# Spectra kept by halves of the channels, products joined in pairs on VectorE, and other first loads, in a long convolution with a sparse feed-forward

## The chip, the cores and the metric

The kernel runs on one core of a Trainium2 chip. The metric is the device time of one execution in microseconds (us), smaller being better. The classes are "faster", "same" and "slower", with a border of 2%. All times below are medians of several executions; the profile is one execution, recorded by the hardware profiler, and its span is about 1.8 us shorter than the device time of that same execution (163.2 of 164.97 us).

## The reference

Two branches work on the same input of 2048 positions and 512 channels, and a gate mixes them. Branch A is a state-space convolution: a kernel of 2048 taps for each channel is built from 128 complex exponentials and applied through a Fourier transform. Branch B sends the two positions with the highest score through a small feed-forward.

```python
def _A_ref(u, A_re, A_im, B_re, B_im, C_re, C_im, log_dt, Dskip):
    dt = jnp.exp(log_dt)[:, None]
    A = A_re + 1j * A_im; Bc = B_re + 1j * B_im; Cc = C_re + 1j * C_im
    P = jnp.exp((dt * A)[:, :, None] * l[None, None, :])          # l = 0 .. 2047, in bfloat16
    K = jnp.einsum("dn,dnl,dn->dl", Cc, P, dt * Bc).real
    ...                                                            # pad to 4096, rfft of K and of u
    y = irfft(Uf * Kf)[..., :L]
    return y.transpose(0, 2, 1) + u * Dskip
def _B_ref(x, w_r, w_gate, w_up, w_down):
    idx = jnp.argsort(-(x @ w_r), axis=-1)[:, :2]
    ...                                                            # silu(xs @ w_gate) * (xs @ w_up) @ w_down, two rows
    return x + upd
x = A_u
g = _sigmoid((x * gate_w).sum(-1, keepdims=True))
return g * _A_ref(x, ...) + (1 - g) * _B_ref(x, ...)
```

## The kernel before

The kernel is written as a graph of named operations. A list scheduler in the program gives each operation an engine (`ENGINE` pins some of them) and a place in that engine's order, after the priorities in `ORDER`; the program is written out with each engine's list in that order. Both tables were searched for, not written by hand. The operations that the argument touches:

The first loads. The sync queue (SP) issues most of them, ScalarE (ACT) two small ones:

```python
g.dma("ld id", ..., writes=[bID], eng=ACT, first=0)      # identity
g.dma("ld ldt", ..., writes=[bLD], eng=ACT, first=1)     # log_dt
for i in range(3):
    for a in range(2):                                   # A_re A_im C_re C_im B_re B_im, all on SP
        g.dma("ld pn%d%s" % (a, "ACB"[i]), ..., 131e3, writes=[bPN[i][a]], first=2 + 2 * i + a)
...                                                      # then u, the transform matrices c_fwd
```

The spectrum X of the input: TensorE (PE) makes two rows at a time, ScalarE or VectorE (DVE) evicts them, VectorE spreads them to sums and differences. A row holds all 512 channels:

```python
def eov(b, ri, row, *dims):
    return tXE(BF, 0, 128, (4 * b + 2 * ri + 1) * 2048 + row * D, *dims)
...
g.op("ev X%d.%d.%d" % (b, ri, pr), {ACT: (... eov(b, ri, 2 * pr, (1, 1024)) ...), DVE: (...)}, bp, [bEO[b][ri][pr]], pref=ACT)
```

The taps of the convolution: decay tables (`t1_...`) are multiplied on VectorE, TensorE makes the taps from them ("tap", lines L898 and L899 of the profile), selections ("sel", L925) and the spectra of the kernel ("Kh", L958) follow, each evicted by ScalarE or VectorE. The products of the spectra come last. Each product of two real planes is one VectorE operation, and so is each sum of two terms; block 1 needs four products a part:

```python
def prod(nm, kb, kri, b, xri, ...):
    tt(nm, lambda: f4(t), lambda: k4(kb, kri), lambda: xw(b, xri), ALU.mult, bKH[...] + bX[b][xri], [bt], cd(NE), bias)
def comb(nm, a, b_, op, dst=None, NE=NE):
    tt(nm, ... a[0] ..., ... b_[0] ..., op, [a[1], b_[1]], [d[1]], cd(NE), bias)
...
ab.append((prod(nm + "a", 0, 0, blk, xs_[0]), prod(nm + "b", 0, 1, blk, xs_[1])))
...
comb(nm, ab[ri][0], ab[ri][1], ALU.subtract if ri == 0 else ALU.add, yds[ri] if blk == 0 else None)
if blk == 1:
    comb(nm + "cd", cd_[ri][0], cd_[ri][1], ALU.subtract if ri == 0 else ALU.add)
    comb(nm + "s", ab[ri][0], cd_[ri][0], ALU.add, yds[ri])
```

Behind them come the folds (VectorE), the inverse transform (TensorE, L1250 to L1254), and the outputs ("out", ScalarE or VectorE), which are stored.

## Time and profile before

| | kernel before |
|---|---|
| time, median of 3 executions | 163.63 us (163.33 to 163.76) |
| the profiled execution | 164.97 us, span 163.2 us |
| busy in it | TensorE and VectorE most: VectorE 149.9 us in 228 instructions |

The profiled execution took 1.2 us more than the longest timed one and 1.3 us more than their median. The lines on which the reading rests stand in the prediction. In a row of the stretches the columns are the bounds, the length, then busy time and number of instructions of PE, PEld (TensorE's weight loads), DVE, ACT and POOL, then the granted clock of TensorE as a share, the share of the DMA engines and GB/s.

### The profile page before, as it was taken

To read this page: it belongs to the slowest core of one execution; us is meant where nothing else is said; L and a number is where in the kernel's file an instruction comes from. 1 tells how busy PE (TensorE), PEld (TensorE's weight loads), DVE (VectorE), ACT (ScalarE), POOL (GpSimd) and SP (SyncE) were. 2 spreads that over 40 slices of the span, in tenths; PEclk is the share of its full clock that TensorE was granted. 3 is DMA by queue.
4 is the path that set the end of the run, shared out by engine and by line. 5 is a ranking of instruction groups with operands and counts; after the bars stand their busy time and mean duration, and the time that the engine had idled before them with its cause. 6 is when DMAs were issued, how large, how long until landed. Compare 5 with 4: busy or idle time off the path is not lost.

```text
span 163.2 us, 3756 instructions
## 1 busy us (share of the span) xinstructions
PE 146.2 (90%) x1574; PEld 102.4 (63%) x1574; DVE 149.9 (92%) x228; ACT 123.8 (76%) x242; POOL 4.2 (3%) x12
## 2 busy tenths in 40 slices
PE   0588899999799999849999999999999999999991
PEld 0443545464334457748555679998588888888880
DVE  0499999999999999999998999999999999999933
ACT  3698999999998998999998989974751602562352
POOL 5000000000000000000100000000000000000000
PEclk9999999999999999858999999999999999999999
DMA  4899600000000996596152504858000000044044
GB/s 148 257 378 416 209 7 0 4 4 0 0 0 3 324 352 227 187 349 242 39 222 38 221 4 159 359 181 335 2 0 6 0 0 4 0 129 133 0 129 129
DMA packets 13300, 21.19 MB, mean 130 GB/s; under 512 B 2018, under 2 KB 10980, under 8 KB 12516
## 3 DMA queue, kind: packets, MB, share of 16 engines
q1 hardware_dynamic: 12996, 20.93, 37.2%
q8 instruction: 12, 0.20, 0.5%
q10 hardware_dynamic: 288, 0.03, 0.1%
q14 instruction: 4, 0.03, 0.1%
HBM read 18.86 MB, written 2.10 MB: 128 GB/s over the span
## 4 chain that ended last, share of the span: by engine, by line
PE 57%; ACT 20%; DVE 16%; DMA 3%; SPq 1%; issue 1%; DVEq 0%
PE RP L1253 17%; PE RP L958 14%; DVE RB L664 10%; PE RP L788 6%; ACT RB L851 6%; ACT RB L768 5%; ACT RB L689 5%; PE RP L844 4%; PE RP L925 4%; DMA RB<-in_A_B_re_dram 3%; PE RP L1250 2%; ACT RB L990 2%; PE RP L1227 2%; PE RP L1147 2%; DVE RB L686 2%; PE RP L898 1%
## 5 line engine op out<-in xcount | busy, mean ns | idle before, releaser
L664 DVE TENSOR_TENSOR RB<-RB 128x2048 bf16<-128x2048 bf16 (+4 forms) x103 | 83.0, 870 | 1.3 <-ACT RB L792 0.8
L844 PE MATMUL RP<-RB 128*128 128x512 bf16 x128 | 31.3, 380 | 2.8 <-ACT RB L851 1.4
L1253 PE MATMUL RP<-RB 128*128 128x256 bf16 x256 | 32.0, 273 | 0.0
L1253 PEld LDWEIGHTS RP<-RB 128*128 128x128 bf16 x256 | 25.0, 98 | 3.0 <-issue 0.2
L958 PE MATMUL RP<-RB 128*128 128x256 bf16 x208 | 25.0, 273 | 0.0
L963 ACT ACTIVATE RB<-RP 128x1024 bf16<-128x1024 f32 x14 | 14.2, 1042 | 13.7 <-PE RP L958 13.7
L708 DVE TENSOR_TENSOR RB<-RB 128x2048 bf16<-128x2048 bf16 x20 | 23.8, 1218 | 0.1
L958 PEld LDWEIGHTS RP<-RB 128*128 128x128 bf16 x208 | 20.1, 98 | 4.5 <-issue 0.2
L844 PEld LDWEIGHTS RP<-RB 128*128 128x128 bf16 x128 | 11.7, 97 | 17.6 <-ACT RB L851 3.3
L1266 ACT ACTIVATE RB<-RP,RB 128x256 bf16<-128x256 f32 x28 | 10.8, 487 | 12.0 <-DVE RB L664 5.5
L792 ACT ACTIVATE RB<-RP 128x512 bf16<-128x512 int16 x32 | 18.4, 610 | 1.5 <-PE RP L788 1.3
L768 ACT ACTIVATE RB<-RP 128x256 bf16<-128x256 f32 x62 | 18.9, 507 | 0.0
L851 ACT ACTIVATE RB<-RP 128x1024 bf16<-128x1024 f32 x15 | 15.4, 1079 | 0.4 <-PE RP L847 0.3
L788 PE MATMUL RP<-RB 128*128 128x512 bf16 x56 | 15.5, 380 | 0.0
L898 PE MATMUL RP<-RB 128*128 128x84 bf16 x128 | 11.8, 213 | 3.5 <-DVE RB L664 3.1
L898 PEld LDWEIGHTS RP<-RB 128*128 128x128 bf16 x128 | 11.2, 105 | 4.0 <-DVE RB L664 3.2
L710 DVE TENSOR_TENSOR RB<-RB 128x1024 bf16<-128x1024 bf16 x20 | 13.4, 683 | 0.0
L899 PE MATMUL RP<-RB 128*128 128x84 bf16 x128 | 11.8, 212 | 0.0
L899 PEld LDWEIGHTS RP<-RB 128*128 128x128 bf16 x128 | 11.3, 105 | 0.0
L689 ACT ACTIVATE RB<-RB 128x512 bf16<-128x512 int16 x16 | 9.1, 626 | 0.5 <-DVE RB L686 0.5
L913 ACT ACTIVATE RB<-RP 128x1008 bf16<-128x1008 f32 x9 | 9.0, 1046 | 0.0
L1250 PE MATMUL RP<-RB 128*128 128x256 bf16 x32 | 8.8, 274 | 0.0
(106 smaller groups left out, 161.1 us busy)
## 6 DMA issues: line engine op xcount, KB each, us to landing
RB<-in_A_u_dram SPq DMA_DIRECT2D x4, 1024.0 KB, 6.0
RB<-c_kspec SPq DMA_DIRECT2D x6, 512.0 KB, 4.6
RB<-c_fwd SPq DMA_DIRECT2D x4, 512.0 KB, 9.1
RB<-c_inv SPq DMA_DIRECT2D x2, 1024.0 KB, 6.6
RB<-in_B_w_up_dram SPq DMA_DIRECT2D x2, 896.0 KB, 6.9
RB<-in_B_w_gate_dram SPq DMA_DIRECT2D x2, 896.0 KB, 6.0
RB<-in_B_w_down_dram SPq DMA_DIRECT2D x2, 896.0 KB, 6.1
out_dram<-RB SPq DMA_DIRECT2D x6, 256.0 KB, 2.4
```

The costliest lines, as they stand in the source:

```text
L664: return g.op(name, {DVE: (lambda h: h.tensor_tensor(out=o(), in0=a(), in1=b(), op=op), cost)}, rd, wr, bias=bias, **kw)
L689: s1.append(g.op("sin z%d.%d" % (t, hh_), {ACT: (lambda h, ta=ta, i=i, hh_=hh_: h.activation(out=tZ[hh_](BF, 0, 128, i * 512, (256, 2), (1 ...
L708: g.op("%s.m%d" % (name, i), {DVE: (lambda h, i=i: h.tensor_tensor(out=ts[i](BF, 0, 128, 0, (n, 2), *like), in0=a_(), in1=b_(i), op=ALU.mu ...
L768: e2.append(g.op("exp t1_%d %d" % (h, m), {ACT: (lambda hh, m=m, s=s, h=h: hh.activation(out=tT1[h](BF, 0, 128, s * 4, (128, NG), (1, 4)), ...
L788: r = hh.matmul(ps(F32, 0, 128, 0, (1, 512)), tAM(BF, 0, 128, 1 * 128, (1, 128)), tU8(BF, 0, 128, (x * 2 + h) * HC, (0, 2), (1, HC)), star ...
L792: sins.append(g.op("sin%d %d.%d" % (h, q, cs), {ACT: (lambda hh, ps=ps, cs=cs, tt_=tt_, q=q: hh.activation(out=tt_(BF, 0, 128, 8 * q, (4, ...
L844: r = h.matmul(o, tF(BF, 0, 128, (((eo * 2 + ri) * 4 + j // 2) * 4 + ft) * 128, (1, 128)), tU(BF, 0, 128, (b * 8 + j) * D, (1, D)), start= ...
L851: g.op("ev X%d.%d.%d" % (b, ri, pr), {ACT: (lambda h, ps=ps, b=b, pr=pr, ri=ri: h.activation(out=eov(b, ri, 2 * pr, (1, 1024)), in_=ps(F32 ...
L898: hh.matmul(o, tT1[h](BF, 0, 128, gr * 128, (1, 128)), t2v(h, 0, 0, (HC, NSL), (1, 4)) if gr == 0 else tT2[h](BF, 0, 128, 4 * gr, (HC, NSL ...
L899: r = hh.matmul(o, tTI[h](BF, 0, 128, gr * 128, (1, 128)), tT2[h](BF, 0, 128, NSL * HC + 4 * gr, (HC, NSL), (1, 4)), start=False, stop=True)
L958: r = hh.matmul(o, tKM[m](BF, 0, 128, c, (1, 128)), tKC[h](BF, 0, 128, u * 256, (1, 256)), start=(n == 0), stop=(n == len(steps) - 1))
L1253: r = hh.matmul(o, tG(BF, 0, 128, ((j * 2 + ri) * 4 + ft) * 128, (1, 128)), SD(hb, ri, ft), start=False, stop=(fin and k == 1 and ft == r0 ...
```

## The change

The intent is fewer VectorE instructions. The two products that a part needs from one kernel block become one operation of double length, and in block 1 the two first sums become one as well. For that the spectra X are kept by halves of 256 channels, so that real and imaginary planes lie at one step (positive for the real part of the product, negative for the imaginary). The first loads are reordered, and `ORDER`, `PLACE` and `ENGINE` are searched anew.

```diff
-        g.dma("ld id", ..., eng=ACT, first=0)
-        g.dma("ld ldt", ..., eng=ACT, first=1)
+        g.dma("ld id", ..., eng=ACT, first=1)
+        g.dma("ld ldt", ..., eng=ACT, first=0)
...
-                g.dma("ld pn%d%s" % (a, "ACB"[i]), ..., 131e3, writes=[bPN[i][a]], first=2 + 2 * i + a)
+                g.dma("ld pn%d%s" % (a, "ACB"[i]), ..., (131e3, 131e3, 200e3)[i], writes=[bPN[i][a]],
+                      eng=ACT if (i, a) == (2, 0) else SP, first=2 + 2 * i + a)
...
-            return tXE(BF, 0, 128, (4 * b + 2 * ri + 1) * 2048 + row * D, *dims)
+            return tXE(BF, 0, 128, (4 * b + 2 * ri + 1) * 2048 + row // 4 * 2048 + row % 4 * HC, *dims)
...
+                        tQ = T(nm, nt * NE * 4); bq = [Buf(tQ) for _ in range(nt)]
+                        for kb in range(nt):
+                            tt(nm + ("ab", "cp")[kb], lambda ...: tQ(BF, 0, 128, kb * 2 * NE, (NE, 2), (NE // 2, 2), (1, NE // 2)),
+                               lambda ...: tKH[h](..., (2048, 2), (4 * HC, 2), (1, NE // 2)),
+                               lambda ...: tXE(..., ((1 - 2 * ri) * 2048, 2), (4096, 2), (1, NE // 2)), ALU.mult,
+                               bKH[h][kb * 4:kb * 4 + 4] + bX[b][0] + bX[b][1], [bq[kb]], cd(2 * NE), bias)
...
+                                tt(nm, lambda qv=qv: qv(0), lambda qv=qv: qv(0), lambda qv=qv: qv(1), op, bq, bq, cd(2 * NE), bias)
+                                tt(nm + "s", yds[ri], ..., ALU.add, bq, [bY[ri]], cd(NE), bias)
...                                    # ORDER and PLACE: all new numbers
-    "ev Kh 0.0.2": DVE, "ev kc1": ACT, "ev X1.0.1": DVE, "ev tap 0.60": DVE, "ev tap 1.60": DVE, "x": DVE, ...
+    "ev Kh 0.1.3": DVE, "ev kc1": DVE, "ev kd0": DVE, "out 0.1.3": DVE, "ev X0.1.0": DVE, "ev X0.1.2": DVE, "x": ACT, ...
```

## The prediction

> **What bounds the kernel now.** I read the busy table by stretches first, then the chain that ended last, then the waits, then the groups by form and single rows of the timeline.
>
> The stretches (time, then busy time and instruction count of each engine, granted clock, DMA share, GB/s):
>
> ```profile
> 8.00:60.00 52.00, 48.26 (x332) 24.30 (x330) 51.64 (x93) 50.33 (x97) 0.31 (x1) 1.00 0.35 128
> 60.00:79.20 19.20, 15.56 (x340) 12.70 (x338) 19.06 (x30) 18.43 (x48) 0.73 (x3) 0.82 0.67 231
> 79.20:158.80 79.60, 79.58 (x884) 63.23 (x885) 75.78 (x102) 49.89 (x91) 0.83 (x3) 1.00 0.29 100
> 158.80:163.20 4.40, 0.83 (x8) 0.49 (x6) 1.75 (x4) 1.24 (x4) 0.00 (x0) 1.00 0.42 119
> ```
>
> The columns after the time are PE, PEld, DVE, ACT, POOL. VectorE works 51.64 of 52.00 us, then 19.06 of 19.20, then 75.78 of 79.60, and the missing 3.8 us of the last figure lie almost wholly behind its final fold at 156.24. ScalarE is as full up to 79 us and then has 30 us to spare. TensorE is not full before 79.2 us, and full after it: 79.58 of 79.60. So there are two bounds on top of each other: VectorE from 8 to 156 us, TensorE from 79.2 to 158.8 us. The chain says the same:
>
> ```profile
> 14.54 5.83 ACT RB L689 x11
> ...
> 63.17 4.41 DVE RB L664 x4
> ...
> 79.00 0.17 DVE RB L1142
> 79.22 3.19 PE RP L1147 x14
> ...
> 157.45 0.33 PE RP L1175 x8
> 157.78 0.99 PE RP L1253 x8
> 158.80 1.36 DVE RB L1271 x3
> 160.16 0.39 DVEq L533
> ```
>
> ScalarE carries it from 14.5 to 48 us, VectorE from 61 to 79, TensorE from 79.22 to 158.8 with no gap. Of the waits, three matter: TensorE for the decay tables that VectorE multiplies, before the first tap (L898); TensorE for a load at the start; VectorE for the first matmuls.
>
> ```profile
> PE RP L898 <- DVE RB L664: 3.1, 1, 3.1
> PE RP L621 <- DMA RB<-in_A_B_re_dram: 1.1, 1, 1.1
> DVE RB L644 <- PE RP L621: 1.1, 1, 1.1
> DVE RB L659 <- PE RP L621: 1.0, 1, 1.0
> ```
>
> What an instruction of VectorE costs, by form (busy us, mean ns) and in a row:
>
> ```profile
> L664 DVE TENSOR_TENSOR RB<-RB 128x2048 bf16<-128x2048 bf16 x49 | 58.0, 1218 | 1.1 <-ACT RB L792 0.6 <-ACT RB L963 0.3
> L708 DVE TENSOR_TENSOR RB<-RB 128x2048 bf16<-128x2048 bf16 x20 | 23.8, 1218 | 0.1
> L664 DVE TENSOR_TENSOR RB<-RB 128x512 bf16<-128x512 bf16 x32 | 12.0, 416 | 0.0
> L664 DVE TENSOR_TENSOR RB<-RB 128x1024 bf16<-128x1024 bf16 x16 | 10.4, 682 | 0.0
> ...
> 107.29 48.95 DVE L664 TENSOR_TENSOR RB<-RB 128x2048 bf16<-128x2048 bf16 x73
> ```
>
> From 682 to 1218 ns are 1024 elements more: 0.523 ns an element. The recorded fixed part, 682 - 1024 x 0.523 = 146 ns, overlaps the neighbour. What a row really pays is in the last line: 73 operations in 48.95 us (its shape is the first one's; it mixes 25 of 2048, 16 of 1024 and 32 of 512 elements, 83,968 together). At 0.521 ns that is 43.7 us of elements, so 5.2 us, or 70 ns an instruction, is the fixed price in a row. L708, whose operands already go in two planes with steps of both signs, has the same 1218 ns.
>
> [...] So joining instructions can save only the 70 ns; no element goes faster. [...] Here one issue on the sync queue takes 0.42 to 0.44 us, so a load moved away lets each later one start by about 0.45 us earlier. [...] a 3.1 us wait ahead of the taps, then 0.75 of the clock in 71 to 79 us.
>
> **The change part by part.**
>
> Products. Each real or imaginary part of a spectrum needs two products for a block, four for block 1. The new code makes the two in one operation of double length. Its first sums of block 1 are also one operation for both kernels' terms. Per pair of half and block:
> - half 0, block 0 and half 1, block 0: per part, two products and one sum become one product and one sum. 2 saved each, 4 together.
> - half 0, block 1: the imaginary part goes from 4 products and 3 sums to 2 and 2 (3 saved). The real part is summed in TensorE and goes from 4 products to 2 (2 saved). 5 together.
> - half 1, block 1: in three pieces, two parts each, 7 to 4 operations: 3 x 2 x 3 = 18 saved.
>
> Sum 27 instructions, so 27 x 0.070 = 1.9 us of VectorE; its elements stay. 1.3 us of it fall into the last block. In the last block VectorE's time (16 operations of 1024, 32 of 512) is 16 x 0.603 + 32 x 0.337 = 20.4 us before and about 19.1 after.
>
> All 27 lie behind about 91 us, where the Y products begin. There TensorE is full too. So by themselves they shorten nothing: TensorE's 79.6 us are the down projection, the remaining sine arguments, selections, kernel spectra, second taps, sums and inverses, and the diff takes no matmul away. The saving reaches the end only through the new order of operations, which is the largest part of the diff. VectorE's work ahead of the first taps includes things for later (the second half's tables, the spreads of X), and 1.9 us of it can be put off behind 79 us. Then the decay tables, and with them TensorE's full stretch, start earlier. ScalarE must keep pace, and it is full there. The assignment list relieves it by two early evictions of X that are now pinned to VectorE where there was one (1.08 us of ScalarE each, 1.21 of VectorE), but adds the copy "x" (0.6 us). So about half of the 1.9 us can be turned into an earlier 79.2: 0.9 to 1.0 us.
>
> Spectra by halves. The evictions of X write four runs of 256 instead of one of 1024, the TensorE add of the previous block reads two runs. Elements stay, I put this at 0. The spreads stay at 2048 contiguous elements.
>
> First loads. log_dt goes before the identity, so the exponential that VectorE and TensorE wait for (4.23 us, 4.97 us) can start up to 0.4 us earlier, but the identity, needed by the same product, comes 0.4 later. B_re goes from fifth on the sync queue (issue at 2.60, needed at 7.05) to third on ScalarE's, at about 1.6. B_im, U and the transform matrices each start some 0.45 us earlier. "x" on ScalarE gives VectorE 0.6 us in its idle start. The head is worth 0.4 to 0.6 us; I take 0.5.
>
> Sum: 163.6 - 1.0 - 0.5 = 162.1 us; I predict 162.1.
>
> **The rivals.**
> - TensorE as the only bound of the last half: VectorE's 1.9 us turn into idle time. For it: 79.58 of 79.60. Against: a wait of 3.1 us and the half clock sit just before that stretch, so its start can move. Then only the head counts: 163.1 us.
> - The whole saving lands: order and assignments were searched anew, VectorE gives 1.9 us, the head 0.5, and the taps meet a warm clock (up to 1.5 us more). For it: the two saturated engines have idle third partners (30 us of ScalarE behind 79). That makes 161.2, and with the clock 159.8.
> - Coarser operations start later: a joined product needs all four evictions of a kernel's spectrum and both parts of X, where one product needed two evictions and one part. The last eviction is about 1.1 us behind. For it: VectorE has waited for an eviction (L963, 0.3 us). Against: VectorE has other products to put in between nearly all the time. If it bites: +0.5 to 1 us, 163.5 to 164.
> - The negative step of the imaginary part's second operand costs the 2x rate. L708 speaks against it. If true, six to eight of the joined products double, over 10 us; I give it 1 in 100.
>
> **Range and chances.** The head is fairly sure, the rest depends on a search that I don't see. 8 in 10: 160.6 to 163.4. Two per cent is 160.4 us, which needs the full saving and the warm clock: 8 in 100. Slower by over 2% (166.9) needs a mistake in the rate: 2 in 100.
>
> **What would show it.** VectorE at about 199 instructions rather than 228, with tensor_tensor forms of 4096 elements at some 2.28 us; the same 0.52 ns an element; its total busy time down from 149.9 by 1 to 2 us. TensorE again without a gap from the down projection to the last inverse, with about 80 us, but starting near 78 rather than 79.2; B_re no longer on the chain. It is wrong if the last stretch of TensorE is itself shorter by a microsecond or more, if the 3.1 us wait before the taps is gone with the clock full, or if VectorE shows new waits for kernel-spectrum evictions.

Its sum: 163.6 - 1.0 - 0.5 = 162.1. Its 1.0 is the estimate of what half of 27 x 70 ns is worth, its 0.5 one from the times of the first loads; the 70 ns and the times are read from the trace. That joining leaves the time of an element as it is was the inference from rows of 512 to 2048 elements; the form of 4096 below has 0.521 ns. "The 2x rate" is the text's name for the 0.52 ns an element of the bf16 forms; with f32 operands the forms of 256 and 512 elements (L759 and L664, 417 and 678 ns) come to 1.02 ns, twice that. "The warm clock" is a granted clock of 1.00 in place of the 0.50 that its trace has from 68.1 to 74.9 us. The "up to 1.5 us" for it comes with no source there. The trace allows such an estimate: 48 taps start at that clock, one each 0.07 us, 3.3 us in all, and at the 0.039 us of the later taps they would take 1.9 us. That a shorter wait brings the full clock was an assumption, not shown.

## The result, and the profile after

| | median | runs | all runs |
|---|---|---|---|
| before | 163.63 us | 4 | 163.33 to 163.76 |
| after | 162.98 us | 4 | 162.91 to 163.25 |

The ratio is 0.9966, with a 95% interval of 0.9948 to 0.9983: "same". A ratio here is the mean time of one kernel's fast runs over that of the other's of the same rounds, so it is not quite the ratio of the medians. The gain is 0.65 us by these medians, and 0.46 us in a second measurement below, where 1.5 had been forecast. The time lies inside the range, but the gain was two to three times too large in the forecast.

The groups by form of the kernel after, VectorE's products and sums (count, busy us, mean ns, idle before):

```profile
L663 DVE TENSOR_TENSOR RB<-RB 128x2048 bf16<-128x2048 bf16 x37 | 44.2, 1219 | 1.0 <-ACT RB L791 0.9
...
L663 DVE TENSOR_TENSOR RB<-RB 128x4096 bf16<-128x4096 bf16 x9 | 20.2, 2287 | 0.0
...
L663 DVE TENSOR_TENSOR RB<-RB 128x1024 bf16<-128x1024 bf16 x16 | 10.3, 686 | 0.0
...
L663 DVE TENSOR_TENSOR RB<-RB 128x512 bf16<-128x512 bf16 x8 | 3.1, 420 | 0.1
```

The double-length form took 2287 ns. From 1219 to 2287 are 2048 elements more, 0.521 ns each, and the longest of the nine took 2290 ns: nothing was lost to the negative steps. VectorE has 201 instructions where it had 228, the 27 that the count gave. Its busy time fell only from 149.9 to 149.4 us, though: 27 instructions at 70 ns are 1.9 us, so some 1.4 us of other work has come to it over the whole kernel.

The same stretches as in the prediction, kernel after:

```profile
8.00:60.00 52.00, 47.42 (x337) 24.80 (x342) 51.42 (x93) 50.97 (x100) 0.59 (x2) 1.00 0.37 132
60.00:79.20 19.20, 15.52 (x327) 12.84 (x326) 19.13 (x27) 18.00 (x46) 0.60 (x3) 0.82 0.50 164
79.20:158.80 79.60, 78.20 (x881) 63.57 (x881) 76.12 (x79) 49.34 (x92) 0.62 (x2) 1.00 0.32 115
...
```

TensorE is done before the third stretch is over, and VectorE has more work in it than before (76.12 against 75.78 us) in 23 instructions fewer (79 against 102). The clock ahead of the taps is as low as it was (0.82). The chain that ended last, kernel after (start, length, what):

```profile
75.64 0.91 ACT RB L913
...
77.73 2.97 PE RP L1147 x13
...
155.66 1.87 PE RP L1236 x16
157.55 0.47 ACT RB L1249
...
```

The down projection (L1147) now follows an eviction of taps on ScalarE (L913), not VectorE. And its waits at the two places that the prediction named:

```profile
DVE RB L606 <- ACT RB L604: 3.8, 1, 3.8
...
PE RP L898 <- DVE RB L663: 2.6, 1, 2.6
```

The wait before the taps is 2.6 us where it was 3.1; no wait for B_re is left. VectorE's last operations, in the timeline of the kernel after (start, length, first of the group, idle before it and what ended it):

```profile
139.67 15.91 DVE L663 TENSOR_TENSOR RB<-RB 128x2048 bf16<-128x2048 bf16 x25
156.24 1.75 DVE L1254 TENSOR_SCALAR RB<-RP,RB 128x256 bf16<-128x256 f32 x4 [0.65 <-PE RP L1236]
```

Before its last outputs VectorE waits 0.65 us for TensorE; before the change that wait was 2.6 us (L1271 in the profile before, 156.24 to 158.80). The two engines end almost together now.

At face value the full stretch of TensorE starts 1.5 us earlier (77.73 against 79.22), more than forecast, while the time fell by 0.65. The two numbers do not fit together, and the reason is the profiled execution of the kernel before.

**Two groups of executions.** The kernel before was run 51 times unchanged in the four calls below. 35 runs took 163.5 to 163.9 us and 16 took 164.4 to 166.3 us (two of these, over 166, carry the label slow; the others are called fast). I call the groups short and long. In the call with the changed kernel itself it was 5 of 11. The profiled execution of 164.97 us, from which the prediction took its positions, is of the long group, and the times that it was to improve on are of the short one. The changed kernel showed no long run in 10. So from here on the kernel before is taken by its short runs alone. A trace of the short group comes from an experiment (before_short), whose program differs from the kernel before only by 14 shortened sums late in the kernel. Its chain:

```profile
78.03 2.97 PE RP L1147 x13
...
```

There the down projection starts at 78.03 and not at 79.22. (The trace has 13 of its 14 matmuls, and so has that of the kernel after; the first weight load of it, which both have, stands at 77.80 and at 77.47.) Against the short group the true gain in that start is 0.3 us (down projection over at 81.00 before, 80.70 after), and the span goes from 161.8 to 161.2.

The first taps, which wait for the decay tables of VectorE, start at the same time in both, first before_short, then the kernel after:

```profile
70.22 0.25 PE L898 MATMUL RP<-RB 128*128 128x84 bf16 x1 [3.06 <-DVE RB L664]
...
70.20 0.25 PE L898 MATMUL RP<-RB 128*128 128x84 bf16 x1 [2.56 <-DVE RB L663]
```

So the wait is shorter because TensorE comes to it later (its work before ends at 67.16 and at 67.64 us), not because the tables come earlier. The 0.6 us of span thus lie behind the first taps: 0.3 us between them and the end of the down projection, and 0.4 us right behind that. There TensorE makes the same 88 selections (L925) and six matmuls of the sine arguments (L788, now L787). Before, they alternate in seven pieces and take 4.97 us (81.36 to 86.33); after, in four pieces, they take 4.57 us (80.62 to 85.19). The first pieces, before_short and then the kernel after:

```profile
81.36 1.65 PE L925 MATMUL RP<-RB 128*32 128x64 bf16 x40
...
80.62 2.14 PE L925 MATMUL RP<-RB 128*32 128x64 bf16 x56
```

From the last matmul to the end of the span the kernel after takes 0.1 us more. This is a reading of the traces; no run changes only these pieces.

### The profile page after: what moved, and what is told of

The parts are those of the page before. It is cut to its first block, busy times and chain, and to the rows that moved or that the text cites. A ratio compares the mean times of both kernels' runs of the same rounds, so it can differ in the third digit from the quotient of the medians.

```text
span 161.2 us, 3720 instructions
## 1 busy us (share of the span) xinstructions
PE 144.4 (90%) x1565; PEld 103.7 (64%) x1574; DVE 149.4 (93%) x201; ACT 122.6 (76%) x242; POOL 4.1 (3%) x12
## 4 chain that ended last, share of the span: by engine, by line
PE 55%; ACT 30%; DVE 10%; DMA 2%; issue 1%; ACTq 0%; DVEq 0%
PE RP L1236 17%; PE RP L958 14%; DVE RB L663 7%; ACT RB L767 7%; ACT RB L850 6%; PE RP L787 5%; ACT RB L688 5%; PE RP L925 4%; ACT RB L990 3%; ACT RB L680 3%; PE RP L1233 2%; PE RP L843 2%; PE RP L1210 2%; PE RP L898 2%; PE RP L1147 2%; PE RP L899 2%
## 5 line engine op out<-in xcount | busy, mean ns | idle before, releaser
L663 DVE TENSOR_TENSOR RB<-RB 128x2048 bf16<-128x2048 bf16 (+5 forms) x76 | 81.3, 1128 | 1.7 <-ACT RB L791 1.4
L843 PE MATMUL RP<-RB 128*128 128x512 bf16 x123 | 30.5, 379 | 3.0 <-ACT RB L850 2.0
L1236 PEld LDWEIGHTS RP<-RB 128*128 128x128 bf16 x256 | 25.0, 98 | 3.1 <-DVE RB L663 0.2
L958 PE MATMUL RP<-RB 128*128 128x256 bf16 x208 | 24.5, 273 | 0.0
L958 PEld LDWEIGHTS RP<-RB 128*128 128x128 bf16 x208 | 20.3, 98 | 4.5 <-ACT RB L936 0.2
L843 PEld LDWEIGHTS RP<-RB 128*128 128x128 bf16 x128 | 12.0, 98 | 17.0 <-ACT RB L850 3.2
L1249 ACT ACTIVATE RB<-RP,RB 128x256 bf16<-128x256 f32 x26 | 10.0, 485 | 13.1 <-PE RP L1175 9.7
L791 ACT ACTIVATE RB<-RP 128x512 bf16<-128x512 int16 x32 | 17.8, 601 | 2.7 <-PE RP L787 2.4
L787 PE MATMUL RP<-RB 128*128 128x512 bf16 x56 | 15.1, 380 | 0.0
L898 PEld LDWEIGHTS RP<-RB 128*128 128x128 bf16 x128 | 11.4, 108 | 3.4 <-DVE RB L663 2.6
L899 PEld LDWEIGHTS RP<-RB 128*128 128x128 bf16 x128 | 11.5, 106 | 0.0
L913 ACT ACTIVATE RB<-RP 128x1008 bf16<-128x1008 f32 (+1 forms) x12 | 10.7, 963 | 0.8 <-PE RP L899 0.8
```

Of the source, the lines that this page charges most:

```text
L663: return g.op(name, {DVE: (lambda h: h.tensor_tensor(out=o(), in0=a(), in1=b(), op=op), cost)}, rd, wr, bias=bias, **kw)
L787: r = hh.matmul(ps(F32, 0, 128, 0, (1, 512)), tAM(BF, 0, 128, 1 * 128, (1, 128)), tU8(BF, 0, 128, (x * 2 + h) * HC, (0, 2), (1, HC)), star ...
L791: sins.append(g.op("sin%d %d.%d" % (h, q, cs), {ACT: (lambda hh, ps=ps, cs=cs, tt_=tt_, q=q: hh.activation(out=tt_(BF, 0, 128, 8 * q, (4, ...
L843: r = h.matmul(o, tF(BF, 0, 128, (((eo * 2 + ri) * 4 + j // 2) * 4 + ft) * 128, (1, 128)), tU(BF, 0, 128, (b * 8 + j) * D, (1, D)), start= ...
L898: hh.matmul(o, tT1[h](BF, 0, 128, gr * 128, (1, 128)), t2v(h, 0, 0, (HC, NSL), (1, 4)) if gr == 0 else tT2[h](BF, 0, 128, 4 * gr, (HC, NSL ...
L899: r = hh.matmul(o, tTI[h](BF, 0, 128, gr * 128, (1, 128)), tT2[h](BF, 0, 128, NSL * HC + 4 * gr, (HC, NSL), (1, 4)), start=False, stop=True)
```

## The experiments

Sixteen kernels ran, in four calls, each call on one chip with 11 executions of the kernel before beside them, six or seven of each kernel. The last column is the median minus that of the short runs of the kernel before in the same call; for variants of the kernel before it takes their own short runs. This column is what the argument uses, since the ratios mix the two groups.

| kernel | call | what it is | median, us | short before, us | difference, us |
|---|---|---|---|---|---|
| after_again | 1 | the changed kernel | 163.11 | 163.57 | -0.46 |
| split | 1 | same order, joined operations issued as two | 164.65 | 163.57 | +1.08 |
| after_oldloads | 1 | three load lines put back | 163.15 | 163.57 | -0.42 |
| before_short | 1 | before, 1.87 us less VectorE late | 163.69 | 163.57 | +0.12 |
| before_again | 2 | the kernel before, for its trace | 163.69 | 163.56 | +0.13 |
| before_loads | 2 | before with the new loads | 163.47 | 163.56 | -0.09 |
| after_ev_act | 2 | three evictions back to ScalarE | 168.27 | 163.56 | +4.7 |
| after_pe_less | 2 | after, 1.74 us less TensorE late | 162.72 | 163.56 | -0.84 |
| before_pe_less | 3 | before, the same less TensorE | 163.15 | 163.62 | -0.47 |
| before_t1_less | 3 | before, 1.07 us less VectorE ahead of the taps | 163.26 | 163.62 | -0.36 |
| after_t1_less | 3 | after, the same less VectorE | 162.68 | 163.62 | -0.94 |
| after_ev_act2 | 3 | the three evictions on ScalarE, placed earlier | 167.09 | 163.62 | +3.5 |
| after_short | 4 | after, 1.87 us less VectorE late | 163.09 | 163.65 | -0.56 |
| after_both_less | 4 | after, less of both late | 162.27 | 163.65 | -1.38 |
| before_both_less | 4 | before, less of both late | 162.59 | 163.65 | -1.06 |
| before_warm | 4 | before, three more warm-up matmuls | 163.65 | 163.65 | 0.00 |

All results passed the comparison with the reference, also those of the kernels that leave work out (their errors stay within its tolerance). For variants of the kernel after, the effect of the edit is the difference in the table minus -0.46.

The theories. TENSOR: TensorE's full stretch from the down projection sets the end, VectorE's saving alone buys nothing, and only an earlier start or a shorter stretch counts. VECTOR: VectorE sets the end in the last block as well. HEAD: the gain comes from the loads.

### after_again: the changed kernel once more

No edit.

> The changed kernel once more, unchanged, as the partner of the next three on the same chip. Every theory expects 0.9966 of the kernel before, within 0.002, and a trace of 161.2 us with TensorE's full stretch from about 77.7 us on.

Six runs took 162.98 to 163.24 us. The ratio of 0.9936 is 0.003 from the expected one and flatters the kernel, since five of the kernel before's eleven runs were long; against the short ones it is 0.46 us. So the gain is between 0.46 and 0.65 us.

### split: the order without the joining

```diff
-    tt(nm + ("ab", "cp")[kb], <4096, 2048 or 1024 elements>)
+    tt2(...)        # the same operation as two tensor_tensor of half the length, one behind the other
-    tt(nm, <both kernels' first sums in one>)
+    tt2(...)
```

> The changed kernel in the same order, but each joined product and joined sum issued as two operations of half the length: 27 instructions of VectorE more, 1.9 us at 70 ns each. Theory TENSOR (TensorE bounds the last half, so the joining is worth little by itself): slower than the changed kernel by 0 to 0.5 us. Rival VECTOR (VectorE is the bound that counts behind 90 us): slower by 1.4 to 1.9 us, so that the order search gave nothing or took something back.

164.65 us: 1.54 us more than the joined version in the same order, and 1.08 us more than the kernel before. 27 more instructions were priced at 1.9 us, so 1.54 of it landed, as the rival VECTOR had it, and the rest, some 0.36 us, was slack of VectorE. The timeline of its VectorE at the end:

```profile
157.78 1.75 DVE L1261 TENSOR_SCALAR RB<-RP,RB 128x256 bf16<-128x256 f32 x4 [0.37 <-PE RP L1243]
```

Two things follow. In the new order VectorE is a bound that lies only a fraction of a microsecond behind TensorE. And the new order and assignment by themselves are worse than the old ones by about a microsecond: they were searched for a VectorE with 1.9 us less to do, and they have given it other work in exchange. Behind 78 us VectorE now evicts kd0, a kernel spectrum (Kh 0.1.3), kc1, a sum (ys 0.1.0.1) and an output (out 0.1.3), about 5.4 us by their durations in the trace, where before it had two evictions of taps and two of kernel spectra, about 3.4. That is 1.9 us, as much as the joining saved. The busy time agrees: from the first weight load of the down projection to the end VectorE is busy for 77.8 us in the kernel after and for 77.7 us in before_warm, an experiment below that was traced in a short run and changes nothing there.

### after_oldloads and before_loads: the loads alone

```diff
 # after_oldloads: kernel after, the three lines back
+identity first, log_dt second on ScalarE; B_re behind C_im on the sync queue
 # before_loads: kernel before with
+log_dt first, identity second, B_re third on ScalarE
```

> The changed kernel with the three load lines of before (identity first, log_dt second, B_re fifth on the sync queue), all else in the same order. If the head is worth what the prediction says: slower than the changed kernel by 0.4 to 0.6 us. Rival (ScalarE and VectorE are fed early enough anyway, the head's gain is swallowed before 14 us): under 0.2 us.

> The kernel before with the new first loads alone (log_dt, identity and B_re issued by ScalarE), all else in its order. Theory: B_re behind four loads on the sync queue is what makes the longer group, so that group is gone and all runs lie between 163.0 and 163.7, at most 0.5 us under the shorter group. Rival: the longer group has another cause (clock, the U load) and appears in about four runs of ten again.

Putting them back cost 0.04 us, bringing them in gave 0.09. HEAD falls: the loads are worth about 0.1 us and not 0.5. Where the half microsecond of the estimate went can be read in the traces: the identity, now issued second, is what VectorE's first product waits for (the chain of the kernel after starts with the load of c_small, 2.50 us, up to 3.65), so log_dt's lead is given back (the table of waits names the exponential of log_dt, which ended at about the same time; its total is 3.8 us and was 3.9 in before_short's trace); and the 1.1 us wait for B_re was a matter of that one long execution. In before_short's trace TensorE's first 12 products follow without a gap at 4.66. One of the six runs of before_loads was long (164.71 us) although B_re was early there, so the late B_re is not what makes a long run either, or not alone.

### before_short and after_short: 1.87 us less VectorE in the last blocks

```diff
 # 14 in-place first sums of block 1 (7 joined ones in the kernel after): 472, 264 or 200 elements of each left out (result wrong on purpose)
+NW = NE - {2048: 472, 1024: 264, 512: 200}[NE]
```

> The kernel before in its own order, wrong on purpose: 14 in-place sums of block 1 leave out 3600 elements together, 1.87 us of VectorE, about what the joining saves and in about the same places. TENSOR: the time stays within 0.4 us of the kernel before, since TensorE is without a gap. VECTOR: faster by 1.4 to 1.9 us.

> The changed kernel, wrong on purpose: its joined in-place sums of block 1 leave out 3600 elements, 1.87 us of VectorE behind 106 us. Later-of-two-ends: TensorE's end is the later one by about 0.36 us, so nothing is gained, 0 to 0.15 us. If the changed kernel is bound by VectorE after all: 1 us or more.

The 1.87 us are an estimate, 3600 elements at 0.521 ns. The kernel before got nothing (+0.12 us), the kernel after 0.1 us at most. Most of the time taken away turned up as idle time. VectorE's timeline in before_short:

```profile
149.52 4.83 DVE L664 TENSOR_TENSOR RB<-RB 128x512 bf16<-128x512 bf16 x15 [0.86 <-PE RP L1254]
157.38 1.75 DVE L1272 TENSOR_SCALAR RB<-RP,RB 128x256 bf16<-128x256 f32 x4 [3.03 <-PE RP L1254]
```

and in after_short:

```profile
156.36 1.75 DVE L1256 TENSOR_SCALAR RB<-RP,RB 128x256 bf16<-128x256 f32 x4 [2.30 <-PE RP L1238]
```

where 0.65 us had been (the row of products ahead of it ends at 154.05 us and not at 155.58). VECTOR falls as the sole bound: in both kernels TensorE sets the end; the kernel before shows VectorE idle for 2.6 us ahead of its last outputs even without the cut.

### before_pe_less and after_pe_less: 1.74 us less TensorE

```diff
 # 16 matmuls of half 1's kernel spectra left out (result wrong on purpose)
-steps = [(u, u, row * 128) for u in range(4)] + ...
+steps = [(u, u, row * 128) for u in range(3 if h == 1 else 4)] + ...
```

> The kernel before with the same 16 matmuls left out (wrong on purpose; 1.74 us of TensorE behind 106 us). Leaving them out of the changed kernel gave 0.35 us, so that one is bound by VectorE. If the kernel before is bound by TensorE, as leaving out 1.87 us of VectorE for nothing says: its shorter group is faster by 1.0 to 1.7 us, until VectorE's last fold becomes the end. If it is a corner of both bounds as well: under 0.4 us.

> The changed kernel, wrong on purpose: half 1's kernel spectra of block 0 leave out one of their terms, 16 matmuls of 256 columns less, 1.74 us of TensorE around 113 to 123 us. If the changed kernel is bound by VectorE: 0 to 0.3 us faster. If TensorE bounds it: 1.3 to 1.7 us faster.

The 1.74 us are an estimate from the chain of the kernel before, where 16 such matmuls in a row (L958) took 1.75 us. The cut gave 0.47 us of 1.74 in the kernel before and 0.38 (0.84 - 0.46) in the kernel after: TensorE is the bound, but only as far as the next engine. Which one that is, the chain of waits of after_pe_less says, by line:

```profile
by line: DVE RB L663 21.7%; PE RP L1236 16.4%; ACT RB L767 6.8%; ACT RB L850 6.2%; PE RP L787 5.2%; ACT RB L688 5.0%; PE RP L958 4.1%; ACT RB L990 2.8%; ACT RB L680 2.5%; PE RP L1233 2.3%; PE RP L843 2.3%; PE RP L925 2.0%; PE RP L1147 1.9%;
```

VectorE's products (L663) went from 6.9% to 21.7% of the span, and the kernel spectra (L958) from 14.2% to 4.1%. So VectorE stands about 0.4 us behind TensorE in the kernel after, the same figure that split gives from the other side.

### before_t1_less and after_t1_less: 1.07 us less VectorE ahead of the taps

```diff
 # half 0: two of eight (seven) factors left out of the products t1r+ and t1r- (result wrong on purpose)
+npl - 2 + 2 * h ... n = 6 + 2 * h
```

> The kernel before, wrong on purpose: four in-place products of half 0's decay tables leave out two of eight planes each, 1.07 us less of VectorE at 61 to 71 us, ahead of the first taps. The prediction's premise is that VectorE's work ahead of the taps sets the start of TensorE's full stretch: then the down projection starts 1 us earlier and the shorter group ends 0.8 to 1.1 us earlier. Rival: ScalarE (exponentials of half 1, tap evictions) or the half clock sets that start: under 0.4 us.

> The same in the changed kernel. It is bound by VectorE at its end and TensorE stands right behind it. If both the premise and the bound hold: 0.8 to 1.1 us faster (VectorE has 1.07 us less, TensorE starts as much earlier). If the start of TensorE's stretch is set by ScalarE: under 0.4 us.

This tests the step on which the forecast rested, that work put off by VectorE ahead of the taps starts TensorE's stretch earlier by as much. The 1.07 us are an estimate, 2048 elements at 0.521 ns; in the traces the two rows of these products take 3.96 and 2.83 us in after_t1_less and 4.49 and 3.36 us in the kernel after, 1.06 us less. The cut gave 0.36 us in the kernel before and 0.48 (0.94 - 0.46) in the kernel after. In the trace of after_t1_less the first taps start at 69.21 instead of 70.20, so nearly the whole saving reaches them (unlike that of the changed kernel itself, whose first taps start where they did before); the down projection ends at 80.40 instead of 80.70, so 0.3 us of it are left there. In between lie the taps and their evictions on ScalarE, for which TensorE waits 0.37 us at 72.7 us. The taps up to 74.8 us start 0.07 us apart in after_t1_less, as they do in the kernel after while the granted clock is 0.50 there (70 to 74 us); at the full clock (74 to 78 us) they start 0.039 us apart.

### after_ev_act and after_ev_act2: three of the evictions back to ScalarE

```diff
 # ev kc1, ev ys 0.1.0.1 and out 0.1.3 from VectorE to ScalarE
+# after_ev_act: by their scheduled time; after_ev_act2: right behind ev kd1, ev kc1 and out 0.1.2
```

> The changed kernel with three evictions that the new assignment puts on VectorE (the first selection of half 1, one summed spectrum, one output; 3.2 us of VectorE) given back to ScalarE, in the same order. If VectorE alone bounds the changed kernel behind 78 us: faster by 1 us or more. If TensorE stands right behind it (a corner of two bounds): 0 to 0.4 us faster. Rival: the evictions come later on ScalarE and TensorE waits for the PSUM they hold: slower.

> The changed kernel with the same three evictions given back to ScalarE as in the failed try, but placed ahead of the 4.8 us of diagonal copies on which TensorE waited there. VectorE has 3.2 us less behind 78 us. If only VectorE bounds: 1 us or more faster. If TensorE stands right behind: 0 to 0.4 us faster, a version that beats both. If PSUM comes free later than on VectorE: slower.

An eviction copies a result of TensorE out of PSUM (RP in the rows, where all its matmuls write). ScalarE has 30 us to spare behind 79 us (busy 49.34 of 79.60), so this should have been free. Against after_again it cost 5.2 and 4.0 us (4.7 and 3.5 in the table, plus 0.46), and the test failed as a test of the saving. Each of the two kernels falls in two groups of its own, two runs of six being 1.5 us or so faster; the trace of after_ev_act is of its slower group, that of after_ev_act2 (165.51 us) of its faster one. What makes these groups was not looked into. The waits of after_ev_act:

```profile
DVE RB L664 <- ACT RB L964: 5.6, 1, 5.6
...
PE RP L959 <- ACT RB L931: 3.1, 1, 3.1
```

ScalarE's list has the diagonals in that place: it makes them from 112.0 to 116.8 us (16 instructions, 4.78 us). The eviction kc1 (L931) landed behind them, at 116.72, and TensorE's kernel spectra and VectorE's products waited. Placed ahead of them, it pushed the diagonals and the evictions of kernel spectra back instead, in the timeline of after_ev_act2:

```profile
114.82 4.78 ACT L1036 ACTIVATE RB<-RB 128x128 bf16<-128x128 bf16 x16
...
119.49 4.73 ACT L964 ACTIVATE RB<-RP 128x1024 bf16<-128x1024 f32 x5
...
127.53 3.56 DVE L664 TENSOR_TENSOR RB<-RB 128x1024 bf16<-128x1024 bf16 x4 [3.46 <-ACT RB L964]
```

So the evictions that the new assignment gave to VectorE are not an oversight: in this order ScalarE is idle on the whole and late in that place. Whether another order, with the diagonals split or earlier, could give VectorE its 1.9 us back was not tried.

### after_both_less and before_both_less: less of both

```diff
 # both cuts in one kernel: the shorter sums and 16 matmuls less (result wrong on purpose)
```

> The changed kernel with both cuts, 1.87 us of VectorE and 1.74 us of TensorE, wrong on purpose. Later-of-two-ends: 1.74 us of TensorE count in full, 1.5 to 1.75 us faster than the changed kernel, though the single cuts gave 0.35 and 0 to 0.15. Independent effects: the sum of the single cuts, at most 0.5 us.

> The kernel before with both cuts, wrong on purpose. Later-of-two-ends: its shorter group is 1.5 to 1.75 us faster, at about 162.0 us, though the single cuts gave 0 and 0.45. Independent effects: at most 0.5 us.

With TensorE and VectorE ending one behind the other, both cuts together should give up to 1.5 to 1.75 us. They gave 0.92 us (1.38 - 0.46) in the kernel after and 1.06 in the kernel before. That is well over the sum of the single cuts (0.1 + 0.38 and 0 + 0.47), so the two engines do stand one close behind the other. It is also short of the full amount, so what the expectation called later-of-two-ends is not the whole rule. The chains show the missing part: they run over VectorE's products up to 125.5 us (after) and some 130 us (before), and from there to the end over TensorE. So a shorter sum should count here only if it lies ahead of that place. One row of VectorE ahead of it differs between the chains, after_pe_less and after_both_less first, then before_pe_less and before_both_less:

```profile
115.38 4.47 DVE RB L663 x3
...
115.60 3.98 DVE RB L663 x3
...
106.00 23.80 DVE RB L664 x24
...
107.14 23.30 DVE RB L664 x24
```

That is 0.49 and 0.50 us of the 1.87: only half 0's sums, 944 elements, lie ahead of the place. Added to what the 16 matmuls gave alone (0.38 and 0.47) it makes 0.87 and 0.97 us, where 0.92 and 1.06 were measured. The rest of the cut became idle time (VectorE waits 1.75 us for TensorE before its last outputs in after_both_less, 0.37 in after_pe_less). So VectorE and TensorE meet in the middle of the last half and not at their ends. The sum fits in both kernels; no run cuts only the sums behind that place.

### before_again and before_warm: what the long runs are

before_again has no edit. before_warm has three more warm-up matmuls in the third group:

```diff
-for k in range(2):
+for k in range(5 if i == 2 else 2):
```

> The kernel before, unchanged. The runs so far fall in two groups, 163.5 to 163.8 and 164.8 to 165.2 us, and the one profile of it lay in the longer group. Expected: both groups again; a trace of the shorter group has a span of 161.8 us, B_re landing about 2.8 us after its issue rather than 4.5, and TensorE's full stretch starting at about 78.0 rather than 79.2.

> The kernel before with three more idle matmuls of 512 columns behind the third warm-up, in the 1.6 us in which TensorE waits for u at 9 to 11 us. If the half clock in the first X rows (5.3 us for 16 matmuls rather than 3.6) makes the longer group: no run over 164.2 us, and the shorter group as before, 163.5 to 163.8. Rival: runs at 164.4 to 166.3 us appear in about a third again.

The trace of before_again fell in the long group (165.34 us). TensorE waits there for the input u and then makes the first rows of X; in its timeline the first of these is

```profile
12.69 5.29 PE L844 MATMUL RP<-RB 128*128 128x512 bf16 x16 [0.66 <-DMA RB<-c_fwd]
```

and in the short execution of before_short

```profile
12.24 3.63 PE L844 MATMUL RP<-RB 128*128 128x512 bf16 x15 [0.72 <-DMA RB<-c_fwd]
```

16 matmuls at 0.33 us against 15 at 0.24, after idle times of the same length (1.60 and 1.62 us for u, 0.66 and 0.72 for the matrix). In the long run TensorE goes at half its clock for part of these rows: the granted clock of before_again is 0.67 in 12 to 14 us, 0.50 in 14 to 16 and 0.98 in 16 to 18, that of before_short 1.00 from 4 to 22 us. before_loads, whose traced run was long too, has rows as slow (5.31 us; 0.83 of the clock in 10 to 20 us), and so have the long runs in the traces of before_t1_less (164.30 us; 5.03) and before_both_less (163.75 us; 15 in 5.31). The length of the waits does not tell the two kinds apart: 1.17 and 0.62 us came ahead of slow rows in before_loads, 1.62 and 0.72 us ahead of fast ones in before_short. The short run in the trace of before_pe_less has the mean clock of before_short, 0.979. The long execution of the prediction is another kind: its clock was full there (1.00 in each stretch of 2 us from 4 to 22 us; 8 matmuls in 1.90 us), and B_re landed late. With the wait filled by warm-up matmuls the timeline of before_warm has

```profile
7.43 3.81 PE L632 MATMUL RP<-RB 128*128 128x512 bf16 x9
...
11.52 3.63 PE L844 MATMUL RP<-RB 128*128 128x512 bf16 x15
```

and none of its six runs was long. The median of the short group did not move (163.65 us both). In that call only one of the kernel before's eleven runs was long, so the six runs prove little by themselves. In the kernel after the rows of X start later, behind the transposes and the warm-ups, and without half clock (1.00 in 14 to 22 us):

```profile
15.58 4.71 PE L843 MATMUL RP<-RB 128*128 128x512 bf16 x21 [0.81 <-ACT RB L990]
```

Counted over all runs, the kernel before was long in 16 of 51, and the kernel after in 0 of 10, and its variants that keep its order and shift no eviction in 0 of 36 (split, old loads, less work; the run furthest from its median lies 0.6 us above it, 163.67 us of after_short). That the new order avoids long runs is therefore well supported; that it does so through the clock in these rows fits seven of the eight traces of the kernel before and its variants, all but that of the prediction, and is suggested, not shown.

## Why the prediction was wrong

1. **Count, rate and price of the joined operations: right.** 27 instructions less, 201 in all, 2287 ns for the long form, 0.52 ns an element, negative steps without loss. split confirms the price: 1.54 of 1.9 us came back when they were undone, and the pe_less pair puts VectorE's slack at about 0.4.
2. **"By themselves they shorten nothing": right.** before_short took the same amount from VectorE in the old order and gained nothing.
3. **The conversion term, "about half of the 1.9 us can be turned into an earlier 79.2: 0.9 to 1.0 us": this step failed.** It needed work of VectorE to be put off from ahead of the taps to behind 79 us. That did not happen: the first taps start at 70.20 us where they started at 70.22, and the start of the down projection moved by 0.3 us, all of it behind the first taps. The search spent the saving otherwise: 1.9 us of evictions went to VectorE behind 78 us. Giving three of them back to ScalarE cost 4.0 and 5.2 us, since ScalarE, by its list, is late there; it was read as having 30 us to spare, and its idle total said nothing about the place. Even a real saving ahead of the taps was worth only a third to a half (1.07 us less gave 0.36 and 0.48). Part of what the step missed came back by a way that it did not have: TensorE's stretch from the end of the down projection to its last matmul is about 0.4 us shorter (80.70 to 157.53 against 81.00 to 158.22). No matmul was moved ahead of it, by the weight loads in the two traces; the 0.4 us are in the first selections, which alternate less with other matmuls. No run isolates this.
4. **The head, "I take 0.5": mis-sized.** Measured 0.04 and 0.09 us.
5. **The base.** 79.2 as the start, the 1.1 us wait for B_re and the 4.23 us wait at the start were read from an execution of the long group, while the time came from the short one. The short group starts at 78.0, has no wait for B_re and 3.9 us in place of 4.23. The head of 0.5 leaned on these. Also, 7.05 us is when B_re landed there; TensorE was waiting for it from 6.01.
6. **The signs.** "Starting near 78" came true, and meant little, since the short group before starts at 78.03. "Busy time down by 1 to 2 us" did not: 0.5. "Wrong if the stretch is shorter by a microsecond or more, or if the wait is gone with the clock full": neither happened; the wait is 2.6 us and the clock 0.82. The prediction names the 3.1 us wait first and the low clock after it. Its own trace has it the other way round: the granted clock is 0.50 from about 68.1 us, while TensorE still works on matmuls of two columns (L1128), and the wait begins at 68.54. In the kernel after it is 67.2 and 67.64. In both the clock was down about 0.4 us before the wait began, so a shorter wait by itself need not have brought a full clock.
7. **Of the rivals,** TensorE as the only bound of the last half, with 163.1 us, gave the measured time almost exactly, in part by luck. Its reasons were only half right: it had the head as the source of the gain, and the head gave a tenth. The rival of coarser operations that start later shows no loss in the trace: the idle before the 4096-element form is 0.0.

The whole gain, then: new order and assignments without joining about +1.1 us, the joining in that order -1.5, the loads within these -0.04; together about -0.5. A faster version than the changed kernel did not come out of the experiments: all that were faster leave out work.

## What to carry to other kernels

When two engines stand within half a microsecond of each other, a saving on one was worth no more than that here. Find the place where one waits for the other, for only what lay ahead of it counted here (0.5 of 1.87 us). The price of a saving must be looked for in what the scheduler or the search moved into the freed time. Look at what stands in an engine's list at the place where its idle time is to be used, not at the total: here three evictions moved to a ScalarE with 30 us of it cost 4.0 and 5.2 us. And compare the profiled execution with the timed ones before taking positions from it: 1.3 us of difference was in view here, and three readings rested on an execution of another kind.
